# Folding a scale into a Gram matrix, moving a clamp to GpSimd, and naming PSUM banks from a rehearsal

## The chip, the cores and the metric

The kernel runs on one core of a Trainium2 chip. The metric is the device time in microseconds (us) of one execution. The core has a matrix engine (TensorE, "PE" in the profile, with its weight loads shown apart as "PEld"), VectorE ("DVE"), ScalarE ("ACT"), GpSimd ("POOL"), and a queue that issues DMAs ("SP"). The engines run side by side, each in its own order, and wait for one another through semaphores.

## The reference, cut to what matters

Two blocks follow one another. `x` is 4 x 12416 x 128, `inducing` is 32 x 128, and the feed-forward width is 1536.

```python
def mab(q, kv):
    s = scale * (q @ kv.transpose(0, 2, 1))
    a = softmax(s)
    return a @ kv
h = mab(I, x)                       # 32 rows for each batch
y = mab(x, h)                       # 49664 rows of 128
rms = sqrt(mean(y * y, axis=-1) + 1e-06)
xn = y / rms * rms_g
out = (silu(xn @ w_gate) * (xn @ w_val)) @ w_out
```

Because `y = a @ h`, the mean square of a row is `a (h hT) aT / 128`. The 32 x 32 Gram matrix `h hT` is therefore enough to normalise a row, and the row itself is never formed.

## The kernel before, in words

**Units and slots.** Each of the 4 batches has 97 tiles of 128 rows. They are grouped into 7 sets (five of 16 tiles, one of 15, one of 2), and the sets into 25 units of mostly 512 columns. A unit meets the feed-forward layer in 12 slots, one for each 128 of the 1536 hidden columns, so that the whole kernel has 1200 slots, 1.35 us each at the time measured. One slot (`slot`) issues a gate product on PE (L716), the SiLU on ACT (L724), a value product on PE (L727) and the product of the two on DVE (L733). The result `u` then goes through the output weights: 411 of the slots as one full fp32 product (L653, `acc<-u,wo`, two passes on PE), and 789 as three products of split operands (L674, L676, and L653 with `more`), which cost additional work on ACT (L698, L702, L707), DVE (L699) and POOL (L703, L708). A string of letters in the kernel says which slot takes which way. In the slots with the letter "s" the product of DVE stays in the value product's PSUM bank until the next slot has split it (L698, L699).

**The seam.** Before a set's units can start, its attention weights `a` are divided by the row's root mean square. That is the function `seam`, eight steps: `turn_a`, `square` (the product with the Gram matrix, L500), `turn_z`, `scale` (L511 sums 32 numbers for each row into a 128 x 16 tile `ms`; L512 multiplies it by 1/128 and clamps it at 1e-6, both on DVE), `root` (L517, the power -0.5 on POOL), `apply` (L521), `turn_b`, `split`. There are 28 seams; one runs ahead of the first slot, and the steps of the other 27 are spread over slots of the set before. The Gram matrix comes from `square_h`, once a batch (L419 on DVE, L421 on ACT), which adds 128e-6 to every number of it.

**PSUM.** [...] Two hold the output sums (`acc`), one the split products (`u`), and five hold everything else: gate and value products, and the products of the attention steps. These five are one pool, `ps_gv`, with one tag "gv" and five buffers, from which the helper `bank()` takes a tile. The framework places each tile when the kernel is built. It does not go round the five in turn: in the program before, 1908 of 2552 successive tiles break the cycle. A product that writes to a bank waits for the last reader of the tile that was there before: ACT for a gate product, DVE for a value product.

**The rehearsal.** Every engine's instructions stand in the order in which the kernel's text issues them. To fix that order, `rehearse()` plays all slots through with a duration for each step (`COST`), keeps an account of when each engine and each of five banks comes free, and decides at which place of which slot an output product is issued (`picks`). Its own inner function `bank()` takes the bank that comes free first by its account. The real `bank()` doesn't know of that choice. Where ACT has to load another table of functions, the rehearsal puts 1.28 us on ACT's account.

Of the kernel before, what the change touches and what calls it, by code (L numbers as in the profile page):

```python
# [9 lines left out]
F32 = mybir.dt.float32  # L10
# [3 lines left out]
AF = mybir.ActivationFunctionType  # L14
ALU = mybir.AluOpType
AX = mybir.AxisListType
PSUM = bass.MemoryType.PSUM

P = 128
# [4 lines left out]
def kernel(  # L24
# [45 lines left out]
    nc = tc.nc  # L70
    B, N, C = x.shape
# [31 lines left out]
    def pool(name, bufs, **kw):  # L103
        return ctx.enter_context(tc.tile_pool(name=name, bufs=bufs, **kw))
# [11 lines left out]
    silp = pool("silp", SILU)  # L116
    up = pool("up", HELD)
    outp = pool("outp", 2)
    ps_gv = pool("ps_gv", 5, space=PSUM)
    ps_acc = pool("ps_acc", 2, space=PSUM)  # L120
    ps_u = pool("ps_u", 1, space=PSUM)

# [61 lines left out]
            nc.tensor.matmul(ps[:, 0:P], ident[:], ident[:], start=True, stop=True)  # L184

    warm(10)
    ps = ps_gv.tile([P, 512], F32, name="gv", tag="gv")
    nc.tensor.transpose(ps[:, 0:m], ind[:], ident[0:m, 0:m])
    nc.vector.tensor_copy(out=indT[:], in_=ps[:, 0:m])

# [94 lines left out]
    sc, gram, stacks = {}, {}, {}  # L285
    flowing = []

    def bank():
        return ps_gv.tile([P, 512], F32, name="gv", tag="gv")

    def attention(b, load_next):

        st = {}
# [115 lines left out]
        def square_h():  # L409

            if not b:
                scale_h()
            stacks[b] = [stk.tile([P, F], F32R, name=n) for n in ("sg", "sv")]
            ps = bank()
            nc.tensor.matmul(ps[:, 0:m], st["hT"][:], st["hT"][:, 0:m], start=True, stop=True)
            for q in range(R):
                to, of_ = gram[b][ts(q, m), ts(q, m)], ps[ts(q, m), 0:m]
                if b:
                    nc.vector.tensor_scalar_add(out=to, in0=of_, scalar1=C * 1e-6)  # L419
                else:  # L420
                    nc.scalar.activation(to, of_, AF.Copy, bias=C * 1e-6)  # L421

        def scores2(s, ps=None):
            ps = ps or scores(s, st["hT"][:, 0:m], quarters[s], per2[s])
# [59 lines left out]
    def seam(b, s):  # L484

        st = {}
        n, rows = per2[s], rows2[s]
        w = n * m
        engine = nc.gpsimd if b or s else nc.vector

        def numbers(name):
            return small.tile([P, 16], F32, name=name)[rows, 0:n]

        def turn_a():
            eT = st["eT"] = work.tile([P, 512], F32, name="eT", tag="work")
            nc.vector.transpose(out=eT[rows, 0:w], in_=sc[b][rows, cols2[s]])

        def square():
            ps = st["ps"] = bank()
            nc.tensor.matmul(ps[rows, 0:w], gram[b][rows, rows], st["eT"][rows, 0:w], start=True, stop=True)  # L500

        def turn_z():
            ps = st["ps"]
            z = st["z"] = work.tile([P, n, m], F32, name="z", tag="work")
            flat = z[rows, :, :].rearrange("p t m -> p (t m)")
            nc.vector.tensor_tensor(out=flat, in0=ps[rows, 0:w], in1=st["eT"][rows, 0:w], op=ALU.mult)
            nc.vector.transpose(out=flat, in_=flat)

        def scale():
            ms = numbers("ms")  # L510
            nc.vector.reduce_sum(out=ms, in_=st["z"][rows, :, :], axis=AX.X)  # L511
            nc.vector.tensor_scalar(out=ms, in0=ms, scalar1=1.0 / C, scalar2=1e-6, op0=ALU.mult, op1=ALU.max)  # L512
            st["ms"] = ms

        def root():
            rs = st["rs"] = numbers("rs")
            nc.gpsimd.tensor_tensor(out=rs, in0=st["ms"], in1=mhalf[rows, 0:n], op=ALU.pow)  # L517

        def apply():
            rs, a = st["rs"], weights(b, s)  # L520
            engine.tensor_tensor(out=a, in0=a, in1=rs.unsqueeze(2).to_broadcast((rs.shape[0], n, m)), op=ALU.mult)  # L521

        def turn_b():
            aT = st["aT"] = work.tile([P, 512], F32, name="aT", tag="work")
            nc.vector.transpose(out=aT[rows, 0:w], in_=sc[b][rows, cols2[s]])

        def split():
            aT = st["aT"]
            hi, lo = split_of[b, s] = [halves.tile([P, 512], F32R, name=k) for k in ("hi", "lo")]
            if b or s:  # L530
                nc.scalar.copy(out=hi[rows, 0:w], in_=aT[rows, 0:w])
            else:
                nc.vector.tensor_copy(out=hi[rows, 0:w], in_=aT[rows, 0:w])
            engine.tensor_tensor(out=lo[rows, 0:w], in0=aT[rows, 0:w], in1=hi[rows, 0:w].bitcast(F32), op=ALU.subtract)

        return [turn_a, square, turn_z, scale, root, apply, turn_b, split]

    def gather(b, u):
# [299 lines left out]
    if B > 1:  # L838
        for _ in range(R):
# [2 lines left out]
    COST = {"turn_x": (0, .63), "scores1": (1.07, .7), "max1": (0, .1), "max2": (.23, .85), "max3": (.2, .1), "turn_e": (0, .63),  # L842
            "exp1_of": (0, 0, 1.14), "sum_h": (2.0, .25), "fold_l": (.16, .15), "divide": (0, .6), "turn_h": (.3, .8),
            "square_h": (.2, .76), "stack": (1.3, 1.32), "scores2": (1.19, .63), "row_max": (0, .59), "sub_max": (0, 0, 0, 1.01),
            "exp2": (0, 0, 1.0), "turn_a": (0, .63), "square": (1.02,), "turn_z": (0, 1.23), "scale": (0, .7),
            "root": (0, 0, 0, 2.9), "apply": (0, 0, 0, 1.01), "turn_b": (0, .63), "split": (0, 0, .51, 1.25),
            "power": (0, .45), "power_number": (0, 0, .63), "upper": (0, .6), "upper_number": (0, 0, .53), "sign": (0, .6),
            "lower": (0, .6, 0, 1.26), "stack_of": (.87, 0, .5), "stack_low": (0, .62), "split_wo": (0, 0, .7, 1.52), "split_last": (0, 0, .35, .65)}
# [122 lines left out]
    def rehearse():  # L971
# [9 lines left out]
        def run(e, us, *after):  # L981
            at[e] = max([at[e]] + [one + 0.04 for one in after]) + us
            return at[e] + TAIL[e]

        def bank():
            return free.index(min(free))

        def soon(k, step):
            later.append([k, step])
# [100 lines left out]
        def slot(b, k, u, j, tanh):  # L1090
            lend(b, k, idle, leaving)
            w = per2[units[u][0]] * m / 512.0
            st = left.setdefault((b, u), dict(left=NJ, three=0, open=0, all=False, slots=0, end=0.0))
            kind = {"s": "sums", "d": "differences"}.get(BLOCKS[b][k])
            first, second = [], []
            picks[b, k] = {0: first, 1: second}
            gi = bank()
            fill(first, free[gi])
            g = run("PE", 0.2325 * w, free[gi])
            silu = run("ACT", 0.5 * w, g, taken[-SILU])  # L1100
            if tanh:
                silu = run("DVE", 0.6 * w, silu)
            free[gi] = silu
            least = (1 if near(b, k, 0, 4) or (b, u) == flat[-1] else 3 if not b and k < 2 * NJ - 8 else
                     RESERVE + 2 * near(b, k, -2, 0))
            choose(second, min(2, max(0, split["all"] - least + 1)))
            if kind != "sums":
                uses[0] += 1
                while queues["plain"] and queues["plain"][0][3] <= uses[0] - HELD:
                    issue("plain", second)  # L1110
            while not idle and any(one[0] == 1 and one[1].__name__ == "three" for one in later):
                issue("three", second)
            vi = bank()
            fill(second, free[vi])
            v = run("PE", 0.2325 * w, free[vi])
            t = run("DVE", 0.6 * w, v, silu)
            taken.append(t)
            free[vi] = 1e9 if kind == "sums" else t
            for one in later:
                one[0] -= 1  # L1120
            while any(not one[0] for one in later):
                one = next(one for one in later if not one[0])
                later.remove(one)
                one[1]()
            for n, (step, args) in enumerate(given(b, k, u, j)):
                if step.__name__ in ("exp1_of", "exp2") and k in plans[b][1]:
                    run("ACT", 1.28)
                do(step, args, picks[b, k].setdefault(n + 2, []))
            if near(b, k, 2, 3):
                run("ACT", 1.28)  # L1130
            if kind:
                kinds[b, u, j] = kind
                st["open"] += 1

                def three():
                    n = idle.pop(0)
                    hi = run("ACT", (0.49 if kind == "sums" else 0.53) * w, t)
                    if kind == "sums":
                        lo = free[vi] = run("DVE", 0.6 * w, hi)
                    else:  # L1140
                        lo = run("POOL", 1.25 * w, hi)

                    def rest():
                        h = hi if kind == "sums" else run("ACT", 0.52 * w, hi)
                        d = run("POOL", 1.25 * w, lo, h)
                        queues["three"].append((d + 0.05, (b, u), w, n))

                    soon(1, rest)

                soon(1, three)  # L1150
            else:
                queues["plain"].append((t + 0.05, (b, u), w, uses[0]))
            split["all"] += 1
            st["slots"] += 1
            if st["slots"] == NJ:
                st["all"] = True
                copy(st, w)
                if not st["left"]:
                    close((b, u), w)
# [69 lines left out]
```

## Time and profile before

| what | time |
|---|---|
| median of 3 runs (1620.89 to 1621.4) | 1620.94 us |
| the profiled execution | 1621.04 us |
| its span, first to last instruction | 1619.1 us |
| PE busy | 1594.3 us, 98% of the span |
| DVE busy | 1454.4 us, 90% |
| POOL busy | 1425.6 us, 88% |
| ACT busy | 1303.6 us, 81% |
| chain of work that ended last: PE's share | 87% |
| L512, the scale and clamp on DVE, 28 times | 20.2 us, mean 720 ns |
| L511, the sum just ahead of it, 28 times | 17.6 us, mean 629 ns |
| L517, the power on POOL, 20 of 28 times on 128 x 16 | 58.4 us, mean 2921 ns |

The profiled execution is 0.1 us over the median, and 1.9 us of it lie outside the span. The first slot starts at 54.4 us; what lies ahead is the first batch's attention, in which PE is kept busy with idle products. "Busy" of PE is the union of its records. Their ends are modelled, so a record covers the waiting in the pipeline too, and the difference of two starts says more than a duration: in the timeline of PE, back-to-back products of split operands with 512 columns start 0.23 us apart, those with 480 columns 0.22 us.

### The profile page before, as it was taken

Reading aid. Unit: us, or ns where it says so; the run is one execution under the profiler, and the core shown is the slowest. Engines: PE = TensorE matmul, PEld = TensorE weight load, DVE = VectorE, ACT = ScalarE, POOL = GpSimd, SP = SyncE. Lnnn points to the kernel's source line nnn. Section 1 sums busy time; section 2 is a strip of 40 time slices with the busy share of each in tenths; the row PEclk is TensorE's granted clock in tenths of the full one; section 3 lists DMA queues with packets and bytes.
Section 4 is the critical chain, followed back from the end, with each engine's and each line's share of the span. In section 5 each row is a group of like instructions: output and inputs, shape, how many; then the busy total and the mean of one; then the engine's idle time right before and its main releaser. Section 6 shows DMA issues by size and latency. Waiting matters only on the chain.

```text
span 1619.1 us, 26069 instructions
## 1 busy us (share of the span) xinstructions
PE 1594.3 (98%) x7169; PEld 1098.3 (68%) x7169; DVE 1454.4 (90%) x2499; ACT 1303.6 (81%) x2461; POOL 1425.6 (88%) x1154
## 2 busy tenths in 40 slices
PE   8999999999999999999999999999999999999998
PEld 6546667756676666776667666676667677777776
DVE  4879988999889998999998999899989999999996
ACT  4678888868887788787888878878788888889886
POOL 1379999999889999999888999899988899999998
PEclk9999999999999999999999999999999999999999
DMA  7455624344362241624344323262221212212111
GB/s 263 92 74 83 117 40 103 84 92 68 62 97 50 44 95 27 134 63 97 65 67 77 64 40 84 51 138 68 57 38 30 40 30 40 40 27 42 37 34 30
DMA packets 389186, 112.57 MB, mean 70 GB/s; under 512 B 365072, under 2 KB 369712, under 8 KB 386480
## 3 DMA queue, kind: packets, MB, share of 16 engines
q1 hardware_dynamic: 388304, 110.82, 34.8%
q8 instruction: 57, 0.93, 0.3%
q14 instruction: 89, 0.73, 0.2%
q10 hardware_dynamic: 736, 0.08, 0.0%
HBM read 53.95 MB, written 27.00 MB: 50 GB/s over the span
## 4 chain that ended last, share of the span: by engine, by line
PE 87%; ACT 3%; DVE 2%; issue 2%; POOL 1%; DMA 0%; SPq 0%; POOLq 0%; ACTq 0%; DVEq 0%
PE acc L653 29%; PE gv L716 17%; PE gv L727 15%; PE u L676 10%; PE u L674 10%; PE gv L323 3%; PE gv L500 1%; PE gv L379 1%; ACT silu L724 1%; DVE u L733 1%; ACT sc L440 1%; ACT xn L698 0%; POOL xn L708 0%; PE gv L454 0%; ACT silu L720 0%
## 5 line engine op out<-in xcount | busy, mean ns | idle before, releaser
L724 ACT ACTIVATE silu<-gv 128x512 f32<-128x512 f32 (+2 forms) x1186 | 687.9, 586 | 162.3 <-PE gv L716 143.9
L708 POOL TENSOR_TENSOR xn<-xn,xn 128x512 fp32r<-128x512 f32 (+2 forms) x605 | 745.2, 1250 | 79.0 <-DVE xn L699 35.5
L727 PE MATMUL gv<-a,sv 128*128 128x512 f32 (+2 forms) x1188 | 602.5, 507 | 2.8 <-DVE u L733 2.4
L716 PE MATMUL gv<-a,sg 128*128 128x512 f32 (+2 forms) x1188 | 487.9, 411 | 8.2 <-ACT silu L724 4.4
L733 DVE TENSOR_TENSOR u<-silu,gv 128x512 f32<-128x512 f32 (+2 forms) x633 | 414.4, 660 | 63.0 <-PE gv L727 33.2
L653 PE MATMUL acc<-u,wo 128*128 128x512 f32 (+2 forms) x822 | 409.7, 581 | 0.6 <-DVE u L733 0.6
L733 DVE TENSOR_TENSOR gv<-silu,gv 128x512 f32<-128x512 f32 (+2 forms) x553 | 367.1, 667 | 39.2 <-PE gv L727 28.0
L716 PEld LDWEIGHTS gv<-a,sg 128*128 128x128 f32 x1188 | 223.6, 188 | 181.1 <-ACT silu L724 42.1
L727 PEld LDWEIGHTS gv<-a,sv 128*128 128x128 f32 x1188 | 223.5, 188 | 128.9 <-issue 41.3
L698 ACT ACTIVATE xn<-gv 128x512 fp32r<-128x512 f32 (+2 forms) x433 | 252.4, 583 | 65.7 <-DVE gv L733 53.8
L699 DVE SCALAR_TENSOR_TENSOR xn<-xn,gv 128x512 fp32r<-128x512 f32 (+2 forms) x433 | 283.9, 656 | 12.5 <-ACT xn L698 6.8
L674 PE MATMUL u<-xn,xn 128*128 128x512 f32 (+2 forms) x581 | 228.7, 394 | 0.0
L703 POOL TENSOR_TENSOR xn<-u,xn 128x512 fp32r<-128x512 f32 (+2 forms) x172 | 216.8, 1261 | 13.3 <-ACT xn L702 13.3
L653 PE MATMUL acc<-xn,more 128*128 128x512 f32 (+2 forms) x581 | 224.5, 386 | 0.6 <-POOL xn L708 0.4
L653 PEld LDWEIGHTS acc<-u,wo 128*128 128x128 f32 x822 | 153.8, 188 | 36.6 <-issue 5.4
L708 POOL TENSOR_TENSOR sv<-sv 128x512 fp32r<-128x512 f32 (+2 forms) x92 | 117.6, 1279 | 10.3 <-DVE sv L699 5.4
L653 PEld LDWEIGHTS acc<-xn,more 128*128 128x128 f32 x581 | 109.1, 188 | 25.8 <-POOL xn L708 3.9
L674 PEld LDWEIGHTS u<-xn,xn 128*128 128x128 f32 x581 | 109.3, 188 | 25.1 <-issue 5.6
L708 POOL TENSOR_TENSOR sg<-sg 128x512 fp32r<-128x512 f32 (+1 forms) x92 | 118.0, 1283 | 7.0 <-PE u L676 2.0
L702 ACT ACTIVATE xn<-u 128x512 fp32r<-128x512 f32 (+2 forms) x172 | 106.2, 617 | 18.4 <-DVE u L733 14.8
L676 PE MATMUL u<-xn,more 128*128 128x512 f32 (+2 forms) x293 | 112.9, 385 | 0.2 <-POOL xn L703 0.2
L676 PE MATMUL u<-xn,xn 128*128 128x512 f32 (+2 forms) x288 | 110.7, 384 | 0.0
(202 smaller groups left out, 1926.3 us busy)
## 6 DMA issues: line engine op xcount, KB each, us to landing
out_dram<-o SPq DMA_DIRECT2D x320, 64.0 KB, 2.0
xT<-in_x_dram SPq DMA_DIRECT2D x60, 256.0 KB, 4.8
xn<-in_x_dram SPq DMA_DIRECT2D x60, 256.0 KB, 5.4
a<-hi SPq DMA_DIRECT2D x156, 64.0 KB, 2.0
a<-lo SPq DMA_DIRECT2D x156, 64.0 KB, 2.0
xn<-in_x_dram SPq DMA_DIRECT2D x5, 1024.0 KB, 10.1
xn<-w SPq DMA_DIRECT2D x18, 256.0 KB, 3.2
out_dram<-o SPq DMA_DIRECT2D x64, 60.0 KB, 2.0
```

Source lines behind the costliest of these rows:

```text
L653: nc.tensor.matmul(acc[:, 0:T], lhsT, rhs, start=st["left"] == NJ, stop=st["left"] == 1)
L674: nc.tensor.matmul(ups[:, 0:T], weight_of(0, j), hi, start=st["k"] == nk, stop=False)
L676: nc.tensor.matmul(ups[:, 0:T], weight_of(1, j), lo, start=False, stop=not st["k"])
L698: nc.scalar.activation(hi, v, AF.Copy, scale=(1.0 - 2.0 ** -13) * 2.0 ** -12)
L699: nc.vector.scalar_tensor_tensor(out=lo, in0=hi.bitcast(F32), scalar=-4096.0, in1=v, op0=ALU.mult, op1=ALU.add)
L702: nc.scalar.activation(d, v, AF.Copy, scale=1.0 - 2.0 ** -13)
L703: nc.gpsimd.tensor_tensor(out=lo, in0=v, in1=d.bitcast(F32), op=ALU.subtract)
L708: nc.gpsimd.tensor_tensor(out=d, in0=hi.bitcast(F32), in1=lo.bitcast(F32), op=ALU.subtract)
L716: nc.tensor.matmul(g[:, 0:T], sg[:, ts(j, P)], a[:, 0:T], start=True, stop=True)
L724: nc.scalar.activation(sl[:, 0:T], g[:, 0:T], AF.Silu)
L727: nc.tensor.matmul(v[:, 0:T], sv[:, ts(j, P)], a[:, 0:T], start=True, stop=True)
L733: nc.vector.tensor_tensor(out=t[:, 0:T], in0=sl[:, 0:T], in1=v[:, 0:T], op=ALU.mult)
```

## The change

It has four parts.

1. The division by 128 goes into the Gram matrix (L419 and L421 scale by 1/128 and add 1e-6 in the same instruction, where they added 128e-6 before).
2. What remains of L512, the clamp at 1e-6, moves from DVE to POOL, into `root`, ahead of the power.
3. The pool of five buffers becomes five tags "gv0" to "gv4" of one buffer each. The rehearsal's `bank()` writes down each number that it chooses, in order, and the real `bank()` takes these numbers one by one. Ahead of the first slot, where nothing is rehearsed, it goes round the five in turn, and the rehearsal's number 0 is the next bank in that turn.
4. The rehearsal's costs change: `scale` from 0.7 to 0.6 us on DVE, a table load on ACT from 1.28 to 1.43 us. The cost of `root` stays. Since the costs decide the places of output products, some of these may move.

```diff
-    ps_gv = pool("ps_gv", 5, space=PSUM)
+    ps_gv = pool("ps_gv", 1, space=PSUM)
...
-    ps = ps_gv.tile([P, 512], F32, name="gv", tag="gv")
+    ps = ps_gv.tile([P, 512], F32, name="gv", tag="gv4")
...
+    BANKS5, turn, turns = 5, [0], []
+
     def bank():
-        return ps_gv.tile([P, 512], F32, name="gv", tag="gv")
+        if turns:
+            n = turns.pop(0)
+        else:
+            n = turn[0] % BANKS5
+            turn[0] += 1
+        return ps_gv.tile([P, 512], F32, name="gv", tag=f"gv{n}")
...
-                    nc.vector.tensor_scalar_add(out=to, in0=of_, scalar1=C * 1e-6)
+                    nc.vector.tensor_scalar(out=to, in0=of_, scalar1=1.0 / C, scalar2=1e-6, op0=ALU.mult, op1=ALU.add)
                 else:
-                    nc.scalar.activation(to, of_, AF.Copy, bias=C * 1e-6)
+                    nc.scalar.activation(to, of_, AF.Copy, bias=1e-6, scale=1.0 / C)
...
             nc.vector.reduce_sum(out=ms, in_=st["z"][rows, :, :], axis=AX.X)
-            nc.vector.tensor_scalar(out=ms, in0=ms, scalar1=1.0 / C, scalar2=1e-6, op0=ALU.mult, op1=ALU.max)
...
-            nc.gpsimd.tensor_tensor(out=rs, in0=st["ms"], in1=mhalf[rows, 0:n], op=ALU.pow)
+            nc.gpsimd.tensor_scalar(out=rs, in0=st["ms"], scalar1=1e-6, scalar2=None, op0=ALU.max)
+            nc.gpsimd.tensor_tensor(out=rs, in0=rs, in1=mhalf[rows, 0:n], op=ALU.pow)
...
-            ... "scale": (0, .7),
+            ... "scale": (0, .6),
...
         def bank():
-            return free.index(min(free))
+            n = free.index(min(free))
+            turns.append((n + turn[0]) % BANKS5)
+            return n
...
-                    run("ACT", 1.28)
+                    run("ACT", 1.43)
...
-                run("ACT", 1.28)
+                run("ACT", 1.43)
```

## The prediction

> **What bounds the kernel now.** I read the page first: the busy line, then the chain of work that ended last.
>
> ```profile
> PE 1594.3 (98%) x7169; PEld 1098.3 (68%) x7169; DVE 1454.4 (90%) x2499; ACT 1303.6 (81%) x2461; POOL 1425.6 (88%) x1154
> ...
> PE 87%; ACT 3%; DVE 2%; issue 2%; POOL 1%; DMA 0%; SPq 0%; POOLq 0%; ACTq 0%; DVEq 0%
> ```
>
> PE bounds it, and none of the edits takes work from PE. So the change can only win what PE loses by waiting. The page's idle columns show little of that (8.2 and 2.8 us before L716 and L727), because a record of PE covers waiting too. I therefore went through the starts of all matmuls in the timeline and laid each behind the one before: 0.4545 ns a column for split operands (0.233 us for 512, as the back-to-back starts show), 0.8375 ns a column and pass for fp32. What starts later than that has waited. Between 54.4 us (first slot) and 1600 us this gives 43.2 us in 291 places of over 30 ns; 2.6 us more in the last 19 us. That is all there is to win: 2.7% of the span, spread over all stages but the last (7.3 us up to 150 us, about 5 us in each 200 us up to 1300, then 1.7 us in 300).
>
> Next, what ends the waits. The chain of waits names PE's weight loads, since the load carries the wait for the PSUM bank:
>
> ```profile
> PEld gv L716 <- ACT silu L724: 43.2, 125, 1.5
> ...
> PEld gv L716 <- DVE u L733: 25.6, 56, 1.9
> ```
>
> Most of this lies under the matmul before (the sums exceed PE's real loss), but the longest, 1.9 us, doesn't. I looked it up in the timelines of DVE, POOL, PEld and PE.
>
> ```profile
> 112.14 0.67 DVE L511 TENSOR_REDUCE ms<-z 128x16 f32<-128x512 f32 x1
> 112.85 0.97 DVE L512 TENSOR_SCALAR ms<-ms 128x16 f32<-128x16 f32 x1
> 113.74 1.27 DVE L733 TENSOR_TENSOR u<-silu,gv 128x512 f32<-128x512 f32 x2
> ...
> 112.52 1.27 POOL L708 TENSOR_TENSOR sg<-sg 128x512 fp32r<-128x512 f32 x1
> 113.90 2.90 POOL L517 TENSOR_TENSOR rs<-ms,mhalf 128x16 f32<-128x16 f32 x1
> ...
> 112.61 0.40 PE L727 MATMUL gv<-a,sv 128*128 128x512 f32 x1
> 114.47 0.50 PE L716 MATMUL gv<-a,sg 128*128 128x512 f32 x1 [1.45 <-DVE u L733]
> ```
>
> L512 handles 16 numbers a partition and takes 0.97 us, longer than the sum over 512 ahead of it. It ends at 113.82, just after POOL's instruction (113.79). The L733 behind it starts 0.9 us late, frees its bank late, and PE stands from 112.85 to 114.47. The other long one, 440.01, is the same: L512 takes 2.02 us there, across two POOL instructions. The answer for the line L512 shows it is the rule:
>
> ```profile
> L512 DVE TENSOR_SCALAR ms<-ms x28: 175/618/2024, 47.0 to 1570.4; 128x16 f32<-128x16 f32 x20, 128x15 f32<-128x15 f32 x4, 32x8 f32<-32x8 f32 x4
> ```
>
> The 175 ns are the one at 47.0 us, where POOL is idle. All 27 others end 21 to 38 ns after an instruction of POOL ends.
>
> [...]
>
> **The change part by part.**
>
> *L512 leaves DVE.* L512 and its gap before (34 ns) cost DVE 0.720 + 0.034 us; 27 times in the slots, 20.4 us of 1454. DVE's own time costs nothing, as it idles 10%. What counts is what stands behind L512: in all cases but a few an L733 or L699, which frees a bank or makes the operand of an output product. PE's waits that start within 5 us after one of the 27 add up to 8.8 us (32 places). Those windows are 8% of the time, so 8% of 43.2, 3.4 us, would lie there by chance. The long ones are 1.62, 1.40, 0.53, 0.49, 0.46, 0.45 and 0.45 us.
>
> *The clamp on POOL.* The trace has no such instruction. POOL's products of L521's form take 1.053 us for 512 columns and 0.999 for 480, so 1.7 ns a column and 0.19 us fixed: 0.21 us for 16 columns. The power takes 2.92 us for 16 and 2.74 for 15, so 0.18 us a column and only some 0.05 us fixed; with that fixed part the clamp would be 0.08 us (below), and at a tenth of the power's price a column on top of 0.05 it would be 0.34 (above). I take 0.2 us, 27 x 0.2 = 5.4 us of POOL's 1425 (2 to 9). Behind it in POOL's queue stand the power and L703 or L708, for which the output products (L653 with `more`, L676) wait. Where POOL used to finish just before L512 could, POOL then stood idle some 0.11 us for the semaphore (113.79 to 113.90 above). That goes, which gives back about a third. PE's waits that POOL ends are few (8 places, 1.7 us, by the semaphore that the matmul carries), so I charge PE 0.4 us. If the cover were gone, it would be the 5.4. Ahead of the first slot nothing hides it, but L512 (0.175) goes and the clamp comes: nought.
>
> *The Gram matrix.* L419 (185 ns, 12 times) and L421 (188 ns, 4 times) stay one instruction each on the same operands: nothing. No DMA is moved.
>
> *The banks.* From the placement of the tiles in the program before, and from when each tile's last reader ends in the trace, I can say for each of 2509 products after 54 us whether its bank was the first to come free. It was 2174 times; the second 310, a later one 25 times. PE's waits sort so:
>
> - bank late, while another had been free for 150 ns or more: 13 waits, 5.4 us, of which 6 (4.6 us) lie within 5 us after an L512. The slips of about 0.1 us at the matmul after such a product (its weights load late) add 1.3.
> - bank late, another free only a little earlier: 8 waits, 4.0 us; half of it could be saved, 2.0.
> - all five in use, after an L512: 0.9. All five in use otherwise: 35 waits, 9.7 us, with 6.5 of slips behind. No choice of a bank helps here.
> - the rest, some 15 us, is not about banks.
>
> Parts 1 and 3 thus treat the same waits: 5.4 + 1.3 + 2.0 + 0.9 = 9.6 us. Without the L512 the banks come free in the order foreseen, and with the rehearsal's numbers a late one is passed over. The rehearsal's durations are those of this trace (0.5 and 0.6 us for ACT and DVE with a tail of 0.1; the trace 0.60 and 0.67), so its order should be near the real one. At worst it is no better than the placement before: nought from this part, and of the 9.6 only what L512 caused, some 5.4 (8.8 less 3.4).
>
> *The costs.* 1.28 to 1.43 us: the trace has 1283 ns for a load, and 1.31 us from the end of the instruction before to the start of the one after, where records otherwise overlap by 0.1, so 1.43 is closer. Eight waits (2.7 us) follow within 4 us of a load; I credit 0.6 us. It also shifts places of output products, which may help or harm: 3 us either way.
>
> *Sum.* -9.6, of which I take nine tenths because a PE that gets ahead meets other waits, -8.6; POOL +0.4; costs -0.6: -8.8 us. From the profiled execution's 1621.04, 1612.2; the median of the runs shown lies 0.1 lower, so **1612 us**.
>
> **Rivals.**
>
> 1. *The rehearsal comes true* (12%). With banks and DVE as it foresees, its placing of output products fills the waits where all five are in use too. For it: 16.2 us of such waits and slips. Against: waits of this kind are also there far from any L512. Two thirds of the 16.2 on top: 1601 to 1603.
> 2. *Given back* (16%). PE gains at the seams and loses it at the next late POOL or ACT result: DVE is 90% busy and POOL 88%, and late in the run POOL is at 95% (143.1 of 150 us from 1450 to 1600). Against: PE loses only 0.5 us in that very stage. Gain 0 to 5: 1616 to 1621.
> 3. *Slower: the numbers from the rehearsal are wrong* (11%). The account drifts from the real course [...], and once it names a bank whose reader is still to come, PE stands, however many others are free. A wrong bank costs 0.4 us now (5.4 in 13). Over about 22 additional ones it outweighs the 8.8; at 40, +7: 1628. For it: the framework's own choice already has the first bank in 87% of cases, so there is more room to lose than to gain. If the two sequences of calls didn't match, every number would be off; but slots and steps issue their tiles in the same order in both, so 1 of these 11%.
>
> **How the numbers follow.** The forecast (1606 to 1616) has 61%. The measurement tells 0.2% apart, 3.2 us, so faster means below 1617.7. Faster: 61 + 12 + 7 of rival 2 = 80%. Same: 8 of rival 2 and 2 of rival 3, 10%. Slower: 1 and 9, 10%. The range that leaves out no more than two in ten goes from 1603 (the lower half of rival 1 outside) to 1620 (rival 3 and a bit of rival 2 outside).
>
> **What would show it.** L512 is gone; L511 is followed at once by L733 or L699. DVE's busy time falls by about 20 us to 1434, POOL's rises by some 5. The clamp takes 0.08 to 0.34 us. PE's longest wait in the slots is under 1.1 us (two of 1.04 at 560.6 and 954.1 us are with all banks in use). PE's waits by starts fall from 43 to about 34 us. The prediction is wrong if PE waits for banks longer than before while other banks are free (rival 3), or if as many waits stand elsewhere, at L653 or L676 for POOL (rival 2).

## The result, and the profile after

The changed kernel takes **1615.95 us** (median of 7 runs, 1614.78 to 1616.44) against 1621.28 us for the kernel before (7 runs, 1620.89 to 1621.96): 0.9966 of the time, 95% interval 0.9955 to 0.9978. That is 5.3 us less, where 9 were forecast. The profiled execution took 1615.95 us.

The page of the changed kernel, its busy line and the shares of the chain that ended last:

```profile
PE 1593.5 (99%) x7169; PEld 1100.1 (68%) x7169; DVE 1438.5 (89%) x2471; ACT 1307.4 (81%) x2461; POOL 1434.7 (89%) x1182
...
PE 83%; POOL 5%; ACT 3%; issue 2%; DVE 1%; SPq 1%; DMA 0%; POOLq 0%; DVEq 0%; ACTq 0%
```

DVE lost 15.9 us of work, POOL got 9.1 more, and POOL's share of the chain rose from 1% to 5%. The lines of the code have moved by 7: the gate product is L723, the value product L734, the DVE product L740, the output product L660, `apply` L528, `turn_b` L532.

The chain of waits of the changed kernel (sum in us, count, longest):

```profile
PEld gv L723 <- ACT silu L731: 38.3, 120, 1.5
...
PEld gv L723 <- DVE u L740: 17.3, 42, 2.7
...
PEld acc L660 <- POOL xn L715: 10.5, 30, 0.9
...
DVE aT L532 <- POOL sc L528: 3.1, 3, 2.5
```

The first two lines are those that the prediction showed, and both fell: 43.2 to 38.3, and 25.6 to 17.3. But the longest wait for DVE grew from 1.9 to 2.7 us, and the waits for POOL rose. DVE's for `apply` was 1.1 us in one place before, and that of the output product for `more` stood in the kernel before as:

```profile
PEld acc L653 <- POOL xn L708: 3.9, 13, 0.6
```

PE's waits worked out from the starts of its products, as in the prediction, fell from 43.2 to 38.2 us between the first slot and 1600 us, and from 2.6 to 2.4 in the tail. Together that is 5.2 us, the measured gain. Sorted by what ends them:

| PE's waits, us | before | after |
|---|---|---|
| bank late, with the slips behind | 27.9 | 16.2 |
| everything else, PE's clock at full speed | 15.3 | 20.4 |
| PE's clock at half speed (below) | 0 | 1.65 |

The bank waits fell by 11.7 us, where the forecast had 9.6 for parts 1 and 3 together. 5.1 came back as other waits, among them products waiting for POOL's `more` (0.96 to 2.88), and 1.65 were lost to something that the prediction did not think of.

**The place where most of it came back.** The timelines of DVE, POOL and PE of the changed kernel, around the first seam, which the prediction showed too (start, duration, engine, instruction; in brackets the idle time before it and what ended it):

```profile
114.52 1.32 DVE L740 TENSOR_TENSOR u<-silu,gv 128x512 f32<-128x512 f32 x2
118.29 0.71 DVE L532 STREAM_TRANSPOSE aT<-sc 128x512 f32<-128x512 f32 x1 [2.45 <-POOL sc L528]
...
113.86 0.25 POOL L523 TENSOR_SCALAR rs<-ms 128x16 f32<-128x16 f32 x1
114.19 2.94 POOL L524 TENSOR_TENSOR rs<-rs,mhalf 128x16 f32<-128x16 f32 x1
117.21 1.05 POOL L528 TENSOR_TENSOR sc<-sc,rs 128x512 f32<-128x512 f32 x1
...
116.76 0.79 PE L734 MATMUL gv<-a,sv 128*128 128x512 f32 x1
119.63 0.50 PE L723 MATMUL gv<-a,sg 128*128 128x512 f32 x1 [2.08 <-DVE u L740]
119.96 1.31 PE L660 MATMUL acc<-u,wo 128*128 128x512 f32 x2
120.42 1.28 PE L734 MATMUL gv<-a,sv 128*128 128x512 f32 x1
121.49 0.63 PE L723 MATMUL gv<-a,sg 128*128 128x512 f32 x1
121.92 1.91 PE L660 MATMUL acc<-u,wo 128*128 128x512 f32 x2
```

And from the kernel before, the same `turn_b` on DVE and the same `apply` on POOL:

```profile
117.96 0.71 DVE L525 STREAM_TRANSPOSE aT<-sc 128x512 f32<-128x512 f32 x1 [1.09 <-POOL sc L521]
...
116.88 1.05 POOL L521 TENSOR_TENSOR sc<-sc,rs 128x512 f32<-128x512 f32 x1
```

The wait at 114.47 is gone, as forecast. DVE, no longer held by L512, runs into `turn_b` early and stands 2.45 us for `apply` (1.09 before), which itself comes 0.33 us later than before because the clamp stands ahead of the power. Behind `turn_b` in DVE's queue are the L740s that free the banks, so PE stands 2.2 us at 119.63. The rehearsal does not know that `turn_b` waits for `apply`. It named a bank whose reader was stuck behind it. By the placement of the tiles, another bank had come free at 117.1, 0.3 us before PE ran out of work at 117.4, and it stayed free through the whole wait. The output product that comes next (119.96) carries no wait of its own in the trace. So with the free bank named, PE could have done the gate product and that one meanwhile, about 1.1 us of the 2.2 (an estimate from their lengths by the starts, 0.23 and 0.86 us); the rest is DVE's lateness. No run tried this alone.

What follows the wait is new: the products after 119.96 are slow themselves. L660 with two passes takes 1.91 us at 121.92, where it took 1.02 before. The answer for stretches of time shows why. Its columns are the stretch, its length, busy time and count of PE, PEld, DVE, ACT and POOL, then PE's granted clock, the DMA share and GB/s:

```profile
113.74:117.15 3.41, 3.41 (x14) 2.11 (x12) 2.10 (x4) 3.10 (x6) 3.22 (x3) 1.00 0.40 36
117.15:120.56 3.41, 1.33 (x6) 0.65 (x4) 2.27 (x4) 1.52 (x3) 3.27 (x3) 1.00 0.01 2
120.56:123.98 3.42, 3.42 (x6) 1.71 (x6) 3.21 (x6) 2.44 (x5) 3.32 (x4) 0.50 0.19 44
```

The last row has a granted clock of 0.50: for 3.41 us after the wait PE had half its clock and got through 6 records, where the stretch ahead of the wait has 14. Half of 3.41 us is 1.7 us of work lost; by the starts it is 1.65. In the kernel before, the clock was whole from 5 us up to 1616 us.

### The profile page after: what moved, and what is told of

Read it like the earlier page. It is cut to its first block, busy times and chain, and to the rows that moved or that the text cites. A ratio compares the mean times of both kernels' runs of the same rounds, so it can differ in the third digit from the quotient of the medians.

```text
span 1614.0 us, 26024 instructions
## 1 busy us (share of the span) xinstructions
PE 1593.5 (99%) x7169; PEld 1100.1 (68%) x7169; DVE 1438.5 (89%) x2471; ACT 1307.4 (81%) x2461; POOL 1434.7 (89%) x1182
## 4 chain that ended last, share of the span: by engine, by line
PE 83%; POOL 5%; ACT 3%; issue 2%; DVE 1%; SPq 1%; DMA 0%; POOLq 0%; DVEq 0%; ACTq 0%
PE acc L660 28%; PE gv L723 16%; PE gv L734 15%; PE u L683 10%; PE u L681 10%; PE gv L330 2%; POOL xn L715 2%; POOL rs L524 1%; PE gv L386 1%; POOL xn L710 1%; PE gv L507 1%; ACT silu L731 1%; SPq L470 0%; ACT sc L447 0%; ACT xn L705 0%
## 5 line engine op out<-in xcount | busy, mean ns | idle before, releaser
L715 POOL TENSOR_TENSOR xn<-xn,xn 128x512 fp32r<-128x512 f32 (+2 forms) x605 | 745.7, 1252 | 70.2 <-DVE xn L706 30.2
L734 PE MATMUL gv<-a,sv 128*128 128x512 f32 (+2 forms) x1188 | 603.3, 508 | 1.3 <-DVE u L740 0.6
L723 PE MATMUL gv<-a,sg 128*128 128x512 f32 (+2 forms) x1188 | 486.3, 410 | 4.6 <-ACT silu L731 2.2
L740 DVE TENSOR_TENSOR u<-silu,gv 128x512 f32<-128x512 f32 (+2 forms) x633 | 414.9, 661 | 68.6 <-PE gv L734 35.5
L660 PE MATMUL acc<-u,wo 128*128 128x512 f32 (+2 forms) x822 | 410.7, 583 | 0.6 <-DVE u L740 0.6
L740 DVE TENSOR_TENSOR gv<-silu,gv 128x512 f32<-128x512 f32 (+2 forms) x553 | 367.7, 668 | 44.1 <-PE gv L734 31.5
L723 PEld LDWEIGHTS gv<-a,sg 128*128 128x128 f32 x1188 | 223.8, 188 | 171.8 <-ACT silu L731 37.2
L734 PEld LDWEIGHTS gv<-a,sv 128*128 128x128 f32 x1188 | 223.8, 188 | 123.4 <-issue 43.1
L706 DVE SCALAR_TENSOR_TENSOR xn<-xn,gv 128x512 fp32r<-128x512 f32 (+2 forms) x434 | 284.5, 655 | 10.5 <-ACT xn L705 5.8
L660 PE MATMUL acc<-xn,more 128*128 128x512 f32 (+2 forms) x581 | 226.4, 390 | 1.9 <-POOL xn L715 1.9
L660 PEld LDWEIGHTS acc<-u,wo 128*128 128x128 f32 x822 | 154.1, 188 | 36.9 <-issue 5.1
L660 PEld LDWEIGHTS acc<-xn,more 128*128 128x128 f32 x581 | 109.0, 188 | 32.1 <-POOL xn L715 10.3
L715 POOL TENSOR_TENSOR sg<-sg 128x512 fp32r<-128x512 f32 (+1 forms) x92 | 118.1, 1283 | 5.5 <-DVE sg L706 1.7
L715 POOL TENSOR_TENSOR sv<-sv 128x512 fp32r<-128x512 f32 (+2 forms) x92 | 118.0, 1282 | 5.4 <-DVE sv L706 2.8
```

What stands on the lines that cost most here:

```text
L660: nc.tensor.matmul(acc[:, 0:T], lhsT, rhs, start=st["left"] == NJ, stop=st["left"] == 1)
L706: nc.vector.scalar_tensor_tensor(out=lo, in0=hi.bitcast(F32), scalar=-4096.0, in1=v, op0=ALU.mult, op1=ALU.add)
L715: nc.gpsimd.tensor_tensor(out=d, in0=hi.bitcast(F32), in1=lo.bitcast(F32), op=ALU.subtract)
L723: nc.tensor.matmul(g[:, 0:T], sg[:, ts(j, P)], a[:, 0:T], start=True, stop=True)
L734: nc.tensor.matmul(v[:, 0:T], sv[:, ts(j, P)], a[:, 0:T], start=True, stop=True)
L740: nc.vector.tensor_tensor(out=t[:, 0:T], in0=sl[:, 0:T], in1=v[:, 0:T], op=ALU.mult)
```

## The experiments

All times are medians, the ratio is to the kernel before on the same chip, and the last column is the ratio times 1621.3 us. The intervals are about 2 us to each side, so differences between two rows are read together with the runs' own ranges.

| kernel | us | ratio [95%] | us to before |
|---|---|---|---|
| the change | 1615.95 | 0.9966 [0.9955, 0.9978] | -5.5 |
| e1: parts 1 and 2 only | 1615.72 | 0.9966 [0.9952, 0.9979] | -5.5 |
| e2: part 3 only | 1619.1 | 0.9985 [0.9979, 0.9992] | -2.4 |
| e3: the change, no clamp on POOL | 1608.49 | 0.9922 [0.9908, 0.9935] | -12.6 |
| e4: e1, clamp on DVE with an accumulator | 1612.93 | 0.9949 [0.9937, 0.9962] | -8.3 |
| e5: the change, clamp as in e4 | 1611.01 | 0.9935 [0.9921, 0.9948] | -10.5 |
| e6: the change, rehearsal told of `apply` | 1612.45 | 0.9943 [0.9931, 0.9956] | -9.2 |
| e7: the change, first `turn_b` later | 1614.4 | 0.9954 [0.9941, 0.9966] | -7.5 |
| e8: the change, old costs | 1613.78 | 0.9953 [0.994, 0.9965] | -7.6 |
| e9: e5 with e7 and the old table cost | 1609.98 | 0.9932 [0.9918, 0.9945] | -11.0 |
| e10: e5 with e6's rule | 1610.48 | 0.9933 [0.992, 0.9945] | -10.9 |
| e11: the change, clamp twice | 1621.08 | 1.0001 [0.9993, 1.0009] | +0.2 |
| e12: the change, old table cost only | 1614.32 | 0.9959 [0.9946, 0.9971] | -6.6 |

e1 to e4 ran together on one chip, e5 to e8 on a second, e9 to e12 on a third.

### The parts alone: e1 and e2

e1 takes the Gram matrix and the clamp, and keeps the one tag with five buffers and the old costs; the diff is against the kernel before.

```diff
-  nc.vector.tensor_scalar(out=ms, in0=ms, scalar1=1.0 / C, scalar2=1e-6, op0=ALU.mult, op1=ALU.max)
...
-  nc.gpsimd.tensor_tensor(out=rs, in0=st["ms"], in1=mhalf[rows, 0:n], op=ALU.pow)
+  nc.gpsimd.tensor_scalar(out=rs, in0=st["ms"], scalar1=1e-6, scalar2=None, op0=ALU.max)
+  nc.gpsimd.tensor_tensor(out=rs, in0=rs, in1=mhalf[rows, 0:n], op=ALU.pow)
```

> The scale in the Gram matrix and the clamp on GpSimd alone; pool of five buffers under one tag and the rehearsal's costs as before. If DVE's wait for GpSimd at L512 is what cost (theory A): the long waits of PE behind the 27 seams go (5 to 8 us by starts), the clamp puts some 0.36 us on GpSimd at each seam, of which PE sees about 2 us, so 3 to 5 us faster than before. If the choice of the banks is what cost (theory B), and L512 only showed it: within 1.5 us of before, with about as many bank waits while another bank is free.

e2 takes the named banks, and keeps L512 and the old costs:

```diff
-        return ps_gv.tile([P, 512], F32, name="gv", tag="gv")
+        if turns:
+            n = turns.pop(0)
...
+        return ps_gv.tile([P, 512], F32, name="gv", tag=f"gv{n}")
...
-            return free.index(min(free))
+            n = free.index(min(free))
+            turns.append((n + turn[0]) % BANKS5)
+            return n
```

> The banks named by the rehearsal alone; L512 on DVE and the costs as before. Theory B: products take the first free bank in 93% of cases as in the changed kernel (87% before), bank waits with another bank free fall from 9.4 to 3 us, 4 to 6 us faster. Theory A: L512 still holds DVE for up to 2 us, which the rehearsal (0.1 us) doesn't know of, the order of freeing is upset there, and the gain is 0 to 2 us.

e1 gives 5.5 us, e2 2.4, and both together with PE's order unchanged (e8 below: on PE its instructions stand in the same order as e2's) 7.6. So the parts nearly add up, as far as intervals of 2 us tell. The prediction had them treat the same waits, 4.6 of the 5.4 us. In e2 the first bank to come free is taken in 93% of the cases (87% before), and yet PE's waits by starts fall only from 43.2 to 40.1. L512 is still there, as e2's answer for its line (L519) shows (min, median, max in ns):

```profile
L519 DVE TENSOR_SCALAR ms<-ms x28: 174/608/2173, 47.1 to 1567.0; 128x16 f32<-128x16 f32 x20, 128x15 f32<-128x15 f32 x4, 32x8 f32<-32x8 f32 x4
```

### Does its form make L512 wait? e4 and e5

The direct trial is another form of the same operation: the clamp stays on DVE, on the same 16 numbers, as a `tensor_scalar` that also writes out its accumulator. That this form would not wait for POOL was assumed until e4 showed it. The accumulator's result is used by nobody. In e4 everything else is as in e1, in e5 as in the changed kernel (with the cost of `scale` at 0.7, since DVE has the clamp again).

```diff
+  nc.vector.tensor_scalar(out=ms, in0=ms, scalar1=1e-6, scalar2=None, op0=ALU.max, op1=ALU.max,
+                          accum_out=small.tile([P, 1], F32, name="mx")[rows, :])
```

> The kernel before (one tag, old costs) with the scale in the Gram matrix and the clamp still on DVE at L512, but in the form that also writes an accumulator. [...] the clamp takes two short rows, 0.2 to 0.4 us together, whatever GpSimd does, and the kernel is 3 to 6 us faster than before. If it is any small instruction behind a reduction that DVE does slowly, the clamp still takes 0.6 to 2 us and the time stays within 1 us.

> The changed kernel with the clamp back on DVE in the form that also writes an accumulator (0.1 us of DVE at each seam), banks named by the rehearsal, scale at 0.7 in its costs. If the named banks and the costs are worth something [...]: 1608 to 1610.5 us, 2.5 to 5 us faster than the same clamp with one tag (1612.9). If the banks are worth nothing: 1612 to 1614.

The answer for L512 in e4:

```profile
L512 DVE TENSOR_SCALAR_CACHE_REDUCE ms<-ms x28: 149/170/171, 47.7 to 1562.1; 128x16 f32<-128x16 f32 x20, 128x15 f32<-128x15 f32 x4, 32x8 f32<-32x8 f32 x4
L512 DVE DVE_READ_ACCUMULATOR ms<-ms x28: 71/82/85, 47.8 to 1562.2; 128x1 f32 x24, 32x1 f32 x4
```

And in the timelines of e4, DVE and then POOL:

```profile
113.52 0.17 DVE L512 TENSOR_SCALAR_CACHE_REDUCE ms<-ms 128x16 f32<-128x16 f32 x1
...
113.18 1.28 POOL L708 TENSOR_TENSOR sg<-sg 128x512 fp32r<-128x512 f32 x1
```

It starts and ends in the middle of POOL's instruction (113.52 to 113.69 us, POOL's from 113.18 to 114.46). No one of the 28 takes over 171 ns, where the plain form took up to 2024 in the kernel before. With that it is shown that L512 was long because its form waited for POOL; what of POOL's it waited for, no trace shows. Removing that wait, with nothing put on POOL, is worth 8.3 us (e4), a good deal more than the 5.4 that the prediction gave L512. e5, which has the named banks and the table cost of 1.43 besides, is at 10.5: 2.2 us more for these two together, a little under the 2.5 to 5 expected, and within the intervals.

### What the clamp costs on POOL: e3 and e11

e3 leaves the clamp out of the computation; e11 does it twice in a row.

```diff
 # e3
-  nc.gpsimd.tensor_scalar(out=rs, in0=st["ms"], scalar1=1e-6, scalar2=None, op0=ALU.max)
-  nc.gpsimd.tensor_tensor(out=rs, in0=rs, in1=mhalf[rows, 0:n], op=ALU.pow)
+  nc.gpsimd.tensor_tensor(out=rs, in0=st["ms"], in1=mhalf[rows, 0:n], op=ALU.pow)
 # e11
   nc.gpsimd.tensor_scalar(out=rs, in0=st["ms"], scalar1=1e-6, scalar2=None, op0=ALU.max)
+  nc.gpsimd.tensor_scalar(out=rs, in0=rs, scalar1=1e-6, scalar2=None, op0=ALU.max)
```

> The changed kernel without the clamp on GpSimd (the clamp is left out; nothing else). If the missing 3.7 us of the forecast were given back through GpSimd (rival 2), the four waits of 0.4 to 0.6 us at the output product 4.2 us behind the power shrink by about 0.35 us each, DVE's wait of 2.45 us for the apply step at 118 us by as much, and the kernel is 2 to 4 us faster than the changed one. If the gain was lost elsewhere: within 0.7 us of the changed one.

> The changed kernel with the clamp done twice on GpSimd (the second on the result of the first, which changes nothing in it). If it is GpSimd's time at the seam that PE pays for: another 0.25 to 0.35 us on GpSimd 28 times, 7 to 10 us, of which PE again sees about three quarters as in leaving the first clamp out: 5 to 8 us slower than the changed kernel. If only what waits just behind the first clamp was hit, or if leaving it out helped by another order: 0 to 3 us slower.

Without the clamp the kernel is 7.1 us faster by the ratios (7.5 by the medians), and a second clamp makes it 5.7 us slower (5.1), which uses up the whole gain of the change. For e3 that is far more than the 2 to 4 us expected. The median runs of the change and of e11 have the same mean clock (0.998), so half clock does not explain what e11 lost. The length of one clamp was forecast well. The answer for its line in the changed kernel:

```profile
L523 POOL TENSOR_SCALAR rs<-ms x28: 230/253/622, 46.9 to 1566.3; 128x16 f32<-128x16 f32 x20, 128x15 f32<-128x15 f32 x4, 32x8 f32<-32x8 f32 x4
```

0.25 us, some 0.09 from its end to the start of the power, and a power that is 0.03 longer (median 2930 ns, before 2899): 0.37 us, 28 times, makes 10 us of POOL. So PE paid for somewhat over half of it (5.1 to 5.7 us for the second clamp; 7.1 to 7.5 for the first, half clock included), not for 0.4 us. PE's waits for POOL in the chains of waits of e3 and of e11 (after: 10.5, 30, 0.9):

```profile
PEld acc L659 <- POOL xn L714: 2.6, 8, 0.6
```

```profile
PEld acc L661 <- POOL xn L716: 13.8, 32, 1.2
```

They rise with the number of clamps. One such place in the timelines of the changed kernel, POOL and then PE:

```profile
620.07 2.93 POOL L524 TENSOR_TENSOR rs<-rs,mhalf 128x16 f32<-128x16 f32 x1
622.97 1.29 POOL L715 TENSOR_TENSOR xn<-xn,xn 128x512 fp32r<-128x512 f32 x1
...
623.47 0.39 PE L683 MATMUL u<-xn,more 128*128 128x512 f32 x1
624.31 0.50 PE L660 MATMUL acc<-xn,more 128*128 128x512 f32 x1 [0.45 <-POOL xn L715]
```

L715, which makes the `more` for an output product, stands behind the power, and PE waits for it. In the four seams where this place recurs, PE's wait 4.2 us after the start of the power is 0, 0.11, 0 and 0.10 us without the clamp (e3), 0.40, 0.61, 0.43 and 0.60 with it (the change), and 0.70, 0.92, 0.73 and 0.93 with the clamp twice (e11). In the kernel before it is at most 0.11 there. So the second clamp, 0.24 us and 0.09 of gap, arrives on PE nearly whole at these places, with 0.30 to 0.33 us.

These places are not all of the price. Between the profiles of e3 and of the change PE's waits by starts differ by 7.2 us: 2.0 at products that wait for a result of POOL, 2.0 between 110 and 130 us (1.65 of it the half clock), and some 3.2 spread over other waits. How the clamp leads to those 3.2 was not traced.

### The first seam: e6, e7 and e10

e6 tells the rehearsal that `turn_b` comes after `apply` and how long clamp and power take. e7 issues `turn_b` and `split` of the first seam two slots and one slot later. e10 is e5 with the first half of e6.

```diff
 # e6 (e10: the second line only)
-  "root": (0, 0, 0, 2.9)
+  "root": (0, 0, 0, 3.25)
-  "apply": "root"}
+  "apply": "root", "turn_b": "apply"}
 # e7
-  (32, 33, 34, 35, 36, 36, 39, 41)
+  (32, 33, 34, 35, 36, 36, 41, 42)
```

> The changed kernel, the rehearsal told what it lacked: turn_b comes after apply, and root takes 3.25 us with the clamp in it, not 2.9. If the gain was lost because the rehearsal names banks and places products by a course in which DVE never waits for the apply step: the 2.2 us of PE at 119.6 us, in which another bank was free, fall under 0.5, and the kernel is 2 to 4 us faster than the changed one. If GpSimd's time itself is what costs: within 1 us of the changed one.

> The changed kernel with turn_b and split of the first seam in the slots two and one slots later. DVE's wait of 2.45 us for the apply step at 118 us falls to under 0.5, and PE's 2.2 us behind it go; with the 1.4 us of waits that follow up to 124 us the kernel is 2 to 3.5 us faster than the changed one. If PE makes up for that wait anyway, because output products are short of operands there: within 0.7 us.

> The clamp on DVE in the form with an accumulator, the banks named, the table load at 1.43, and the rehearsal told that turn_b comes after apply. If what it is told is what helped by 3.5 us in the changed kernel: 1607 to 1609.5. If it only drew another order of output products: anything between 1609 and 1613.

e6 was meant to do away with PE's wait at 119.6, and that failed: the rehearsal only moves output products, `turn_b` stays at its place in DVE's queue, and PE still stands 1.7 us at 120.1. Yet the kernel is 3.5 us faster than the change. e7 does move the instruction. DVE's wait for `apply` falls from 2.5 us to 0.4 at most, but PE stands 1.18 us at 126.0 instead, for the DMA that brings the next `a`, since `split` comes a slot later. 1.5 us are gained by the medians, 2.0 by the ratios, at or under the lower end of the 2 to 3.5 expected, and about what the half clock alone took. With the clamp off POOL, the rule is worth nothing that can be told (e10 against e5: 1610.48 and 1611.01, ranges 1609.46 to 1610.50 and 1610.48 to 1611.58).

Part of e6's gain is the clock. The answer for stretches of e6:

```profile
117.26:120.67 3.41, 1.86 (x6) 0.86 (x5) 2.51 (x5) 1.60 (x3) 3.33 (x4) 1.00 0.01 2
120.67:124.08 3.41, 3.41 (x13) 2.16 (x12) 3.41 (x6) 2.61 (x5) 3.31 (x4) 1.00 0.24 58
```

PE stood for 1.81 of the first 3.41 us by the starts (1.55 by its busy time, since a record covers waiting), and no half clock follows. Of e6's five runs, the two of 1613.2 us have a mean granted clock of 0.998, the profiled one of 1610.74 has 0.999.

### The costs: e8 and e12

```diff
 # e8 (e12: the table load only)
-  "scale": (0, .6)
+  "scale": (0, .7)
-  run("ACT", 1.43)
+  run("ACT", 1.28)
```

> The changed kernel with the rehearsal's costs as before (scale 0.7, table load 1.28). If part 4 brought what was forecast: 0.6 us slower than the changed one, with more waits behind the table loads. If it only moves output products about: anything from 2 us faster to 2 us slower.

> The changed kernel with the table load at 1.28 in the costs, scale left at 0.6. If the 1.43 is what makes the new costs 2 us worse than the old ones: about 1613.8, as with both costs old. If the 0.1 us at scale does it: about 1616. If every shift of the costs just draws another order: between 1612 and 1618, and no rule.

With the old costs the kernel is 2.2 us faster than the change (runs 1613.46 to 1614.69 against 1614.78 to 1616.44). The new costs don't help; they take about a quarter of the gain (2.1 us by the ratios). Where, is again in the first seam: between 110 and 130 us PE waits 4.1 us in the changed kernel and 2.1 in e8, and in every other stage the two agree within 0.6. The same DVE wait (2.43 us) makes PE stand 1.63 us in e8 and 2.22 in the changed kernel, as the output products stand at other places in PE's order. And e8's stretches show no half clock behind it:

```profile
117.83:121.24 3.41, 1.93 (x7) 0.95 (x6) 2.85 (x5) 1.71 (x3) 3.33 (x4) 1.00 0.08 19
121.24:124.65 3.41, 3.41 (x14) 2.17 (x12) 3.41 (x7) 2.71 (x6) 3.31 (x3) 1.00 0.18 43
```

0.6 of longer wait and 1.65 of half clock are the 2.2 us. e12, which takes back the table's cost alone, lies between the two (runs 1613.92 to 1615.04, its profile with no half clock at the seam) and can't be told from e8. So most of the loss comes with the 1.43, and the 0.6 at `scale` does little. But the 1.43 is no price as such: e5 has it too, and no half clock. With the clamp on POOL it draws an order of output products in which PE stands 2.32 us of one 3.41 us stretch at the first seam (1.74 in e12), and half a clock follows.

### The edge of the clock

The half clock was not foreseen, so I laid PE's waits over the clock's records of all profiles. In each trace the granted clock changes only at whole multiples of 3.413 us from its first record (the half clock of the changed kernel begins 34 of them after it, those of e11 14 and 34), so I sorted the waits by a grid of that step. One step of the grid is called a cell here. The table has the cell in which PE stood longest by the starts while the slots run, and what came in the next cell:

| profile | cell, us | PE stood, of 3.41 | next cell |
|---|---|---|---|
| e8 | 117.8 | 1.73 | whole |
| e12 | 119.2 | 1.74 | whole |
| before | 438.4 | 1.78 | whole |
| e6 | 117.3 | 1.81 | whole |
| the change | 117.2 | 2.32 | half |
| e11 | 119.4 | 2.56 | half |

And the stretches of e11, the grid's two cells:

```profile
119.36:122.77 3.41, 1.03 (x5) 0.67 (x4) 2.29 (x4) 1.53 (x3) 3.30 (x3) 1.00 0.00 0
122.77:126.18 3.41, 3.41 (x6) 1.67 (x5) 3.18 (x6) 2.41 (x5) 3.31 (x4) 0.50 0.19 45
```

By these six the edge lies between 1.81 and 2.32 us of standing in one cell. Three early half clocks narrow it: e1, e11 and e12 each also show one in the cell around their first slot (from 55.2, 54.5 and 54.3 us), after the load phase. For the load phase PE's idle time is taken from the stretches, a stretch's length less PE's busy time, which gives less than the starts, since a record covers waiting: 1.55 us for e6's cell of the table, 2.08 for the change's, 2.38 for e11's. e1's two cells:

```profile
51.74:55.16 3.42, 1.85 (x12) 1.33 (x12) 3.12 (x5) 0.18 (x1) 0.03 (x1) 1.00 0.07 16
55.16:58.57 3.41, 3.41 (x12) 2.79 (x11) 1.49 (x3) 2.02 (x4) 1.38 (x2) 0.50 0.43 100
```

That is 1.57 us idle ahead of the half clock; in e12 it is 1.58 and in e11 1.92, while in the other eleven traces no cell ahead of the slots is idle for more than 1.44 us, and the clock there stays whole. Over all cells of the fourteen traces, from the clock's first record until the slots end, every one with 1.57 us or more is followed by half a clock and none with 1.55 or less. So by PE's busy time the edge lies between 1.55 and 1.57 us in these traces. (In the last cells, where the work runs out, one of 1.49 was also followed by half a clock.)

In the changed kernel one gap of 2.2 us, which fell whole into one cell (117.15 to 120.56 us), stands ahead of the half clock. What a wait that straddles two cells does was not shown. Where the grid lies differs between the profiles: the clock's first record is at 4.9 us in the kernel before and at 4.5 in the changed kernel. Six runs of the changed kernel have a mean clock of 0.998, the seventh, the fastest (1614.78, 1.2 us under the median of the six), 0.999. That this seventh was spared is inferred from its mean, not seen.

### A version that beats both: e9

e9 takes the clamp in e4's form, the named banks, `turn_b` of the first seam as in e7, and both old costs.

```diff
+  nc.vector.tensor_scalar(out=ms, in0=ms, scalar1=1e-6, scalar2=None, op0=ALU.max, op1=ALU.max,
+                          accum_out=small.tile([P, 1], F32, name="mx")[rows, :])
...
-  nc.gpsimd.tensor_scalar(out=rs, in0=st["ms"], scalar1=1e-6, scalar2=None, op0=ALU.max)
...
-  "scale": (0, .6)
+  "scale": (0, .7)
...
-  (32, 33, 34, 35, 36, 36, 39, 41)
+  (32, 33, 34, 35, 36, 36, 41, 42)
...
-  run("ACT", 1.43)
+  run("ACT", 1.28)
```

> All that helped by itself together: the clamp on DVE in the form with an accumulator, the banks named, the costs before (scale 0.7, table load 1.28), turn_b and split of the first seam two and one slots later. If the gains add: 1621 less 8.4 (the clamp in that form), less 2.3 (banks), less 1 to 2 (turn_b), 1608.5 to 1610.5. If they treat the same waits, as the clamp with the banks and the later turn_b might: 1611 to 1613.

1609.98 us, 11.0 us less than before and 6 less than the change, and it computes all of the reference. e5 and e10 are within about 1 us of it. Only e3, which has no clamp at all, is faster: the clamp on DVE costs PE some 2 us (e5 against e3, by the ratios, less than the width of their intervals).

## Why the prediction was right, and where it was not

The forecast of 1612 us was 4 us too low; 1615.95 lies in the range (1603 to 1620), at the upper end of the 1606 to 1616 that had 61%, and below the 1617.7 under which the prediction counted it as faster (80%). By its steps:

**L512 leaves DVE: right that it waited for POOL, too small.** L512's plain form waited for POOL (in e4's form it takes 171 ns at most), and the wait at 114.47 went. The prediction counted PE's waits within 5 us behind an L512, less those there by chance: 5.4. (Its windows are 27 x 5 us of the 1546 us in which the waits were counted, 8.7% and not 8%, so this sum should have been 5.0.) Taking that wait away while leaving the work on DVE gave 8.3. That the windows of 5 us missed what a late DVE does further on is likely, but not shown. DVE's busy time fell by 15.9 us, not 20: L512's record overlaps that of the next instruction (112.85 and 0.97 us against a start at 113.74), and busy time is a union.

**The clamp on POOL: right in the length of one, wrong in its price.** 0.25 us lies in the forecast's 0.08 to 0.34. But POOL's busy time rose by 9.1 us, where 5.4 (2 to 9) was forecast, and the idle time that was to go in exchange stayed: POOL still stands 0.09 us ahead of the clamp (113.77 to 113.86), and 0.08 more ahead of the power. The step that failed most is "I charge PE 0.4 us". It was read from the eight places where POOL ended a wait of PE *before*. But those show only how often POOL was already late, not how little it lacked to be late. The prediction named the other end itself, 5.4 us "if the cover were gone"; a second clamp cost 5.1 to 5.7, and the first 7.1 to 7.5, half clock included. Where the price could be traced, there was no cover: behind the power stands L715, and in the four seams above PE waited for it almost one for one. This term alone is larger than the whole miss.

**The Gram matrix: nothing**, and no run speaks against it: its two lines take 186 and 189 ns in the changed kernel, 185 and 188 before. It wasn't tried alone.

**The banks: right in direction.** The first free bank is taken in 93% of the cases (87% before), a third or later one in 2 cases (25 before). PE's bank waits fell by 11.7 us, forecast 9.6 for parts 1 and 3 together. Alone, the named banks gave 2.4 us (e2). What was wrong is that this part and the first treat the same waits: they nearly add up.

**The costs: wrong sign.** -0.6 was credited and 3 us either way allowed; they cost 2.2 (e8 against the change), of which 1.65 is the half clock.

**The sum.** Without the clamp on POOL the change gives 12.6 us (e3), where the prediction had 9.2 for the same terms (8.6 and 0.6). With it, 5.5. Two terms were too small, one on each side, and partly cancelled; that the total came near is owed to that, and so to luck.

**The rivals.** Rival 2, "given back" at the next late POOL result, is what the runs show in good part: PE's own loss at products that wait for POOL rose from 0.96 to 2.88 us (L660's waits for `more` from 3.9 to 10.5). The prediction gave it 16% and put it at 1616 to 1621; the result stands at its edge. Its objection, that PE loses little in the stage where POOL is at 95%, was beside the point: what counted here was not POOL's share but what is queued behind its longest instruction. Of rival 3 two places are seen: by the prediction's own sorting, the waits for a late bank while another had been free for 150 ns or more fell from 13 (5.4 us) to 2, but these two are long, 0.66 us at 60.3 and 2.22 at 119.6. The second is the longest wait of the slots and just what this rival described, a bank named whose reader is still to come; some 1.1 us of it is owed to the choice, by the estimate above. Rival 1 did not come true: of 16.2 us of waits and slips with all five banks in use, 12.8 are still there.

**What would show it.** "The longest wait is under 1.1 us" failed: 2.2 at 119.6. "PE's waits fall to about 34" failed: 38.2, of which 1.65 is not waiting. POOL's busy time rose by 9.1 us and not by some 5, and DVE's fell to 1438.5 and not to 1434.

What stays open: what of POOL's the plain form of L512 waits for, by which waits some 3 us of the clamp's price reach PE, what naming the free bank at 119.6 would have given, why e6 gains more than its half clock explains, whether the half clock falls in the same cell in all six runs with a mean of 0.998, and why the new costs leave PE 0.6 us less to do at the first seam.

## What to carry to other kernels

Before moving even a quarter of a microsecond to an engine that looks idle for a tenth of the time, look at what is queued behind it there and how much slack each consumer has, not at how often that engine is late today; the slack can be measured by doing the small step twice. When an engine's instruction waits for another engine's, look first for a form of the same operation that does not: here that was worth 3 to 5 us more than moving the work (e4 against e1, e5 against the change). An engine set free can run earlier into its next wait (DVE stood 2.45 us for `apply` here, 1.09 before), so after each removed wait ask which instruction in its queue now waits, and what stands behind it.

## What the runs showed of the hardware

- In the fourteen traces PE's granted clock changes only at whole multiples of 3.413 us from its first record. While the slots run and in the load phase ahead of them, every cell of that length in which PE's records leave 1.57 us or more idle is followed by a cell at half clock (granted clock 0.50), and none with 1.55 us or less. In the changed kernel a single wait of 2.2 us stands ahead of such a cell, which cost 1.65 us more.
- On DVE, `tensor_scalar` on 128 x 16 numbers or fewer takes 149 to 171 ns in the form with an accumulator, and 71 to 85 ns for reading that out, in all 28 places (e4); the plain form took 175 to 2024 ns in the kernel before, and in 27 of 28 places ended 21 to 38 ns after an instruction of POOL.
- On POOL, a `tensor_scalar` maximum on 128 x 16 takes 0.25 us, a twelfth of the power on the same tile (2.93 us). The first one in the run took 0.62.
